# Last modes by column halves, moved identity passes, two more weight loads by fours, and 8 of 18 output items in 4 KB rows

## The chip, the cores and the metric

The kernel runs on one core of a Trainium2 chip. The core has five engines that follow their own instruction streams and wait for each other by semaphores: TensorE (PE, matrix products into the accumulators called PSUM), VectorE (DVE), ScalarE (ACT), GpSimd (POOL) and SyncE (SP). Transfers between device memory and on-chip memory run on 16 DMA engines; they are issued by instructions on the queues of POOL, SP or ACT. Here POOL issues nearly all loads, because they turn 32-bit inputs into 16-bit data on the way, and SP issues all stores. The metric is the device time in microseconds of one execution; less is better.

## The reference

Two parts follow each other. First a sparse attention over 8 batches, 8 heads, 576 positions and 64 columns per head. Heads 0 to 3 look at the last 32 positions, heads 4 to 7 at the earlier positions with the same remainder modulo 32:

```python
mask_local = (rel >= 0) & (rel < stride)
mask_strided = (rel >= 0) & (pos[None, :] % stride == pos[:, None] % stride)
...
attn = np.exp(scores)
attn = attn / (np.sum(attn, axis=-1, keepdims=True) + 1e-09)
return np.matmul(attn, v).astype(np.float32)
```

Its output, x with 8 x 576 rows of 512 columns, goes through a spectral mix. The first 64 Fourier modes of x along the positions are each multiplied by a complex 512 x 512 matrix of their own, the result y is added, and a last product with a positive part is added too:

```python
X = np.fft.rfft(x, axis=1)
Yr = np.einsum('bmd,mde->bme', Xr, w_r) - np.einsum('bmd,mde->bme', Xi, w_i)
Yi = np.einsum('bmd,mde->bme', Xr, w_i) + np.einsum('bmd,mde->bme', Xi, w_r)
Y[:, :n_modes] = Yr + 1j * Yi
y = np.fft.irfft(Y, n=S, axis=1)
u = x + y
return (u + np.maximum(u @ w_ch, 0.0)).astype(np.float32)
```

The mode matrices are 2 x 64 x 512 x 512 numbers of 32 bits, 134 MB of reading. The output is 9.4 MB.

## The kernel before, in words

**Order of work.** The program writes out the order of every engine by hand. Strided attention of all batches comes first, then local attention of all batches (a loop over b, L850), into which the first modes are woven: `NMODES` of them per batch, 14 with batch 0. Then comes a stretch with the other modes, and at the end the inverse transform and the output.

**Modes and their two halves.** A mode is computed in two passes, one over the channels of each attention half. `mode(slot, m)` (L618) does mode m of one half. Slot 0, and slot 1 up to mode 47, go in pairs through `mode_pair` (L589), with the weights streaming through PE (the matmuls of L601). The last 16 modes of slot 1 go singly with the weights held and X streaming: 16 matmuls of L634 per mode, four column blocks e times four channel blocks c. Eight modes share one PSUM bank `y`. When the bank is complete, `spectrum` (L563) adds it on DVE into the tile `YT` (L567); for the last bank this happens in two parts, after modes 61 and 63.

**Weights.** `w_fetch` (L161) issues the loads of mode weights on POOL: w_r into partitions 0 to 63, w_i into 64 to 127. The unit is a pair of modes, 512 KB for w_r and 512 KB for w_i. The pairs live in a ring `wring` with room for five; three of the first eight pairs (`GUEST`: 1, 2 and 7) live in other tiles and give no ring place back. A pair of numbers in the set `QUADS` (L153) is loaded with the following pair in one go (four modes, 1 MB each for w_r and w_i) as soon as two places are free; the set starts at 13. `UNEVEN` splits a few loads into row counts that spread differently over the DMA engines. A load waits on POOL until PE has used the weights whose place it takes, and POOL works in order. The eight first pairs are issued during strided attention. From then on each use of a pair that is in the ring calls w_fetch once.

**Tail.** With the last bank in YT, `spec_z` (L742) multiplies the last 16 modes by w_ch (four matmuls into zp; ACT copies it to `zzs`), and eight transposes bring the same modes into yp (DVE copies them to `yys`). Earlier modes have by then been folded into kept partial sums: v0s (product with w_ch) and xos (without), by `renew`. The output is made in 18 items k, each 512 KB. For an item, `v_early` (L994) and `u_early` (L1002) pass the kept sums through PE with an identity matrix into PSUM; `new_rows` (L1009) adds the last modes, by matmuls that use only 32 of the 128 rows of the PE array, row group b % 4 for batch b; `v_done` (L1036) takes the positive part on ACT; `u_done` (L1048) adds both on DVE and issues the store on SP. In items 4, 5 and 6 (`pooled`, L999) POOL adds one kept half in place of PE. The identity passes of items 0 and 1 (two v_early, one u_early) stand after mode 62, by `late[22]` (L1062).

**Items.** Items 0 to 15 take a pair of batches and one of four sets t of 128 rows: t % 2 is the parity of the row number, t // 2 the first or second half of the rows. A partition holds one row of 2 KB for each of the two batches, and a store writes rows of 2 KB that lie 4 KB apart (`out_rows`, L1022). Items 16 and 17 take the 64 remaining rows of four batches each. Items 0, 4, 5 and 6 are added and stored in two halves (`pieces`).

Of the kernel before, what the change touches and what calls it, by code (L numbers as in the profile page):

```python
# [10 lines left out]
FP = mybir.dt.float32  # L11
F16 = mybir.dt.float16
# [6 lines left out]
DM = 512  # L19
NM = 64  # L20
# [36 lines left out]
def kernel(  # L57
# [10 lines left out]
    nc = tc.nc  # L68
    PSUM = bass.MemoryType.PSUM
# [5 lines left out]
    pss = {}  # L75
# [10 lines left out]
    def psum(kind, half=False, pair=False):  # L86
        if pair:
            return pss[kind].tile([128, 2, 512], FP, tag=kind, name=kind)
        if half:
            return pss[kind].tile([128, 1024], F16, tag=kind, name=kind)  # L90
        return pss[kind].tile([128, 512], FP, tag=kind, name=kind)
# [19 lines left out]
    idn = cs["cI"]  # L111
# [6 lines left out]
    Xh = {1: big.tile([128, 4, B, 2, NM], F16, name="X1")}  # L118

    YS = {}  # L120
# [29 lines left out]
    ORDER = [(1, m) for m in range(SPLIT1)] + [(0, m) for m in range(SPLIT0)]  # L150
    ORDER += [(1, m) for m in range(SPLIT1, NM)] + [(0, m) for m in range(SPLIT0, NM)]
    UNEVEN = {64: (25, 12, 27), 84: (6, 54, 4), 94: (10, 54)}
    QUADS = {p for p in range(13, 54) if (p - 13) % 5 in (0, 2)}  # L153
    wring = pw.tile([128, 2 * NWBUF, 4, DM], F16, tag="w", bufs=1, name="wring")
    w_tiles = []
    w_chs = {}
# [4 lines left out]
    def w_fetch(n=1):  # L161
        free_pairs[0] += n
        while len(w_tiles) < 2 * NM:
            i = len(w_tiles)
            pair = i // 2
            nm = 4 if pair in QUADS else 2
            if 2 * free_pairs[0] < nm:
# [86 lines left out]
    def act_copy(out, in_):  # L254
        nc.scalar.activation(out=out, in_=in_, func=ACTF.Copy)  # L255
# [300 lines left out]
    ypt = {}  # L556
    queued = []

    def flush():
        while queued:  # L560
            queued.pop()()

    def spectrum(slot, part, src):  # L563
        if slot == 0:
            nc.scalar.activation(out=YS["Y0"][part], in_=src, func=ACTF.Copy)
        else:
            nc.vector.tensor_tensor(  # L567
                out=YS["YT"][part], in0=src, in1=YS["Y0"][part], op=AluOp.add
            )
# [48 lines left out]
    def mode(slot, m):  # L618
        half = 1 - slot
        if m % 2:  # L620
            flush()
        if slot == 0 or m < SPLIT0:
            if m % 2:
                mode_pair(slot, m - 1)
            return
        mi, mg = m % 8, m // 8
        if mi == 0:
            ypt[slot] = psum("y")
        yp = ypt[slot]
        yv = yp.rearrange("p (m e x) -> p m e x", m=8, e=4)  # L630
        wt = w_tiles[ORDER.index((half, m))]
        for e in range(4):
            for c in range(4):
                nc.tensor.matmul(  # L634
                    yv[:, mi, e, :],
                    wt[:, XC[c], ds(128 * e, 128)],
                    Xh[half][:, c, :, :, m],
                    start=(c == 0),
                    stop=(c == 3),
                )  # L640
        if m % 2:
            w_fetch()
        ends = {5: 6, 7: 2} if mg == 7 else {7: 8}
        if mi in ends:
            n = ends[mi]
            m0 = mi + 1 - n
            spectrum(
                slot,
                (slice(None), slice(None), mg // 2, slice(None), ds(8 * (mg % 2) + m0, n)),
                yp.rearrange("p (m e x) -> p e x m", m=8, e=4)[:, :, :, ds(m0, n)],  # L650
            )
# [90 lines left out]
    def spec_z(g, bq, zp):  # L742
        for e in range(4):
            lhs = YS["YT"][:, e, g, ds(8 * bq, 8), :].rearrange("p x m -> p (x m)")
            nc.tensor.matmul(
                zp, lhs, w_chs["n"][:, e, :], start=(e == 0), stop=(e == 3)
            )
# [56 lines left out]
    first = str_front(0)  # L804
# [45 lines left out]
    for b in range(B):  # L850
# [3 lines left out]
        ends = [lambda h=h: loc_scores(b, h, True) for h in (0, 2)]  # L854
# [8 lines left out]
        n = 0  # L863
        nm = NMODES[b]
        for mi in range(nm):
# [3 lines left out]
            n = upto  # L869
# [8 lines left out]
    zzs = [ptr.tile([128, DM], F16, name=f"zz{i}") for i in range(B)]  # L878
    yys = [ptr.tile([128, DM], F16, name=f"yy{i}") for i in range(B)]
# [22 lines left out]
    for b in range(B + 1):  # L902
        for t in range(5):
            if b > 0 and (t < 4 or b % 2 == 0):
                work.append(lambda b=b, t=t: premix(b - 1, t))
            if b < B and t < 4:
                half, cp = ((1, 0), (1, 1), (0, 0), (0, 1))[t]
# [3 lines left out]
    A3 = cs["cFl"].rearrange("p a t m -> p (a t m)")[:, 0 : S + 128]  # L911
# [25 lines left out]
    n = 0  # L937
    for m in range(SPLIT0):
# [4 lines left out]
        n = upto  # L943
# [7 lines left out]
    def spec_late(mm, kept, eng):  # L951
        up = psum("p", pair=True)
        for bq in range(2):
            mm(2, bq, up[:, bq])
        for b in range(B):
            eng(kept[b][64:96], up[ds(32 * (b % 4), 32), b // 4])
# [19 lines left out]
    late = {0: [lambda: spec_late(spec_z, zzs, act_copy)], 1: [spec_last]}  # L976
    for n, i in enumerate([3, 5, 7] + list(range(8, 21))):
        b, t = n // 2, n % 2 * 2
# [3 lines left out]

    items = []
    for P0 in (0, 2):
        items += [((2 * P, 2 * P + 1), t) for t in range(4) for P in (P0, P0 + 1)]
    items += [(range(b, b + 4), 4) for b in (0, 4)]
    LAST = len(items) - 1
    vps, ups, rls, osbs = {}, {}, {}, []

    def own(item, kept, half):  # L990
        bs, t = item
        return [kept[b][:, t] for b in bs] if t < 4 else [half[b // 2] for b in bs[::2]]

    def v_early(k):  # L994
        vps[k] = psum("p", pair=True)
        for j, r in enumerate(own(items[k], v0s, v0h)):
            nc.tensor.matmul(vps[k][:, j], idn, r, start=True, stop=False)  # L997
# [4 lines left out]
    def u_early(k):  # L1002
        ups[k] = psum(("p", "u")[k % 2], pair=True)
        for j, r in enumerate(own(items[k], xos, xoh)):
            if pooled(k, j):
                continue
            nc.tensor.matmul(ups[k][:, j], idn, r, start=True, stop=False)

    def new_rows(k, acc, spectra):  # L1009
        bs, t = items[k]  # L1010
        for j, b in enumerate(bs):
            q = ds(32 * (b % 4), 32)
            i = j // 2 if t == 4 else j
            o, cols = acc[:, i], row_cols(b, t)
            if t == 4:
                o = acc[ds(64 * (b % 2), 64), i]
            fresh = spectra is yys and pooled(k, i)
            nc.tensor.matmul(  # L1018
                o, A3[q, cols], spectra[b // 4][q], start=fresh, stop=True
            )  # L1020

    def out_rows(b, t):  # L1022
        if t < 4:
            steps = [[2 * DM, 128], [(S + 64) * DM, 2], [1, DM]]
            first = 256 * (t // 2) + t % 2
        else:
            steps = [[DM, 128], [2 * S * DM, 2], [1, DM]]
            first = 512
        return bass.AP(
            tensor=out.tensor, offset=out.offset + (S * b + first) * DM, ap=steps  # L1030
        )
# [14 lines left out]
                )  # L1046

    def u_done(k):  # L1048
        bs, t = items[k]
        up, rl = ups.pop(k), rls.pop(k)  # L1050
        if not osbs:
            osbs.append(pw.tile([128, 2 * NWBUF, 2, DM], FP, tag="w", bufs=1, name="osb"))
        osb = osbs[0][:, k % (2 * NWBUF)]
        for j in pieces(k):
            nc.vector.tensor_tensor(
                out=osb[:, j], in0=up[:, j], in1=rl[:, j], op=AluOp.add
            )
            nc.sync.dma_start(out_rows(bs[0], t)[:, j], osb[:, j])

    flush()  # L1060
    rest = [(0, m) for m in range(SPLIT1, NM)] + [(1, m) for m in range(SPLIT0, NM)]
    late[22] = [lambda: v_early(0), lambda: v_early(1), lambda: u_early(0)]  # L1062
    for i, (slot, m) in enumerate(rest):
        mode(slot, m)
        for w in late.get(i, ()):
            w()
    yctx.close()
    with tc.tile_pool(name="ps_s", bufs=1, space=PSUM) as pss["s"]:
        zp = pss["s"].tile([128, 512], FP, name="zp")
        yp = pss["s"].tile([128, 2, 512], F16, name="yp")  # L1070
        spec_z(3, 0, zp)
        act_copy(zzs[0], zp)
        for bq in range(2):
            for e in range(4):
                lhs = YS["YT"][:, e, 3, ds(8 * bq, 8), :].rearrange("p x m -> p (x m)")
                nc.tensor.transpose(yp[:, bq, ds(128 * e, 128)], lhs, idn)
        for bq in range(2):
            nc.vector.tensor_copy(out=yys[bq], in_=yp[:, bq])
    pss["u"] = pctx.enter_context(tc.tile_pool(name="ps_u", bufs=1, space=PSUM))

    for k in range(2):
# [1 line left out]
    for k in range(2):  # L1083
        v_done(k)
    for k in range(2):
        if k:
            u_early(k)
        new_rows(k, ups[k], yys)
        u_done(k)
    for k in range(2, LAST + 2):  # L1090
        if k == 7:
            held = psum("p", pair=True)[:, 0]
            spec_z(3, 1, held)
            act_copy(zzs[1], held)
        if k <= LAST:
            v_early(k)
        if k > 2:
            u_early(k - 1)
        if k <= LAST:
            new_rows(k, vps[k], zzs)  # L1100
        if k > 2:
            new_rows(k - 1, ups[k - 1], yys)
        if k <= LAST:
            v_done(k)
        if k > 2:
            u_done(k - 1)
# [31 lines left out]
```

## Time and profile before

| | |
|---|---|
| time, median of 3 runs | 425.84 us (425.5 to 427.29) |
| the profiled execution | 425.88 us, span 424.1 us |
| PE busy | 340.9 us (80%) |
| DVE busy | 234.6 us (55%) |
| ACT busy | 219.0 us (52%) |
| POOL busy | 95.7 us (23%) |
| software queue (POOL's loads) | 24624 packets, 81.28 MB, 96.7% of 16 engines' span |
| hardware queue (SP's stores and two small loads) | 5248 packets, 9.65 MB, 6.2% |
| stores | 14 of 512 KB and 8 of 256 KB |

How to read it. The profile is one execution. "Busy" is time in which an instruction of the engine ran. The page's slices cut the span into 40 equal parts. In the order of time a row is: start and duration in us, engine, line of the kernel, operation, tile written <- tiles read, shapes, count of merged instructions, and in brackets how long the engine had been idle before and what ended that. The windows table gives for each stretch the busy time of every engine, the granted share of PE's clock, the share of DMA engines at work and the GB/s that landed on chip (16-bit data; what is read from memory is twice that for the weights).

### The profile page before, as it was taken

Reading aid. Unit: us, or ns where it says so; the run is one execution under the profiler, and the core shown is the slowest. Engines: PE = TensorE matmul, PEld = TensorE weight load, DVE = VectorE, ACT = ScalarE, POOL = GpSimd, SP = SyncE. Lnnn points to the kernel's source line nnn. Section 1 sums busy time; section 2 is a strip of 40 time slices with the busy share of each in tenths; the row PEclk is TensorE's granted clock in tenths of the full one; section 3 lists DMA queues with packets and bytes.
Section 4 is the critical chain, followed back from the end, with each engine's and each line's share of the span. In section 5 each row is a group of like instructions: output and inputs, shape, how many; then the busy total and the mean of one; then the engine's idle time right before and its main releaser. Section 6 shows DMA issues by size and latency. Waiting matters only on the chain.

```text
span 424.1 us, 9718 instructions
## 1 busy us (share of the span) xinstructions
PE 340.9 (80%) x4164; PEld 206.5 (49%) x4164; DVE 234.6 (55%) x469; ACT 219.0 (52%) x391; POOL 95.7 (23%) x165
## 2 busy tenths in 40 slices
PE   2987878769999298889874959895779979989993
PEld 2866767554656155556542425453344534535331
DVE  3788788950354134545323326864385646555794
ACT  1687678642666056565753323622162365534772
POOL 7332333322422011102122101212111232310200
PEclk9999899967999789999998789999798998989999
DMA  8999999999999999999999999999999999997598
GB/s 147 211 212 213 213 212 214 210 212 210 214 214 211 215 216 213 214 215 214 211 215 213 212 211 216 213 213 214 213 214 211 214 214 214 213 213 145 196 380 316
DMA packets 30347, 91.62 MB, mean 216 GB/s; under 512 B 3873, under 2 KB 4641, under 8 KB 30305
## 3 DMA queue, kind: packets, MB, share of 16 engines
q0 software_dynamic: 24624, 81.28, 96.7%
q1 hardware_dynamic: 5248, 9.65, 6.2%
q8 instruction: 32, 0.52, 0.5%
q10 hardware_dynamic: 432, 0.08, 0.1%
q14 instruction: 11, 0.08, 0.0%
HBM read 162.83 MB, written 9.44 MB: 406 GB/s over the span
## 4 chain that ended last, share of the span: by engine, by line
PE 46%; DMA 23%; DVE 17%; ACT 8%; issue 4%; POOL 1%; DVEq 0%; ACTq 0%; POOLq 0%
DMA wring<-in_moe_w_i_dram 22%; PE y L601 11%; PE sc L726 5%; DVE xb L245 3%; ACT X L255 3%; DVE kz L287 3%; DVE yy L761 2%; PE p L997 2%; PE tp L417 2%; PE y L536 2%; PE sc L536 2%; PE sc L463 2%; PE p L769 2%; PE p L1018 1%; ACT PL L493 1%
## 5 line engine op out<-in xcount | busy, mean ns | idle before, releaser
L601 PE MATMUL y<-wring,X 128*32 128x512 f16 (+1 forms) x424 | 65.8, 422 | 23.6 <-DMA wring<-in_moe_w_i_dram 23.6
L190 POOL DMA_DIRECT2D wring<-in_moe_w_r_dram x39 | 23.6, 606 | 204.3 <-PE y L601 180.6
L601 PEld LDWEIGHTS <-X 128*32 128x32 f16 (+1 forms) x448 | 27.5, 139 | 41.4 <-DMA wring<-in_moe_w_i_dram 24.3
L735 ACT ACTIVATE v<-sc 128x512 f16<-128x512 f32 x32 | 19.1, 597 | 45.4 <-PE sc L726 45.4
L736 DVE COPY xo<-tp 128x512 f16<-128x512 f16 x32 | 22.1, 691 | 36.5 <-PE tp L734 36.4
L255 ACT ACTIVATE yr<-y 128x512 f16<-128x512 f32 x28 | 16.7, 597 | 41.2 <-PE y L601 41.0
L726 PE MATMUL sc<-w_cp,xT 128*128 128x512 f16 x128 | 36.2, 404 | 1.9 <-DVE xT L694 1.9
L245 DVE TENSOR_TENSOR xb<-av,rec 90x256 f16<-90x256 f32 (+2 forms) x80 | 36.0, 450 | 2.8
L493 ACT ACTIVATE PL<-sc 128x480 f16<-128x480 f32 (+1 forms) x48 | 26.9, 578 | 20.1 <-PE sc L479 19.8
L244 DVE RECIPROCAL rec<-av 90x4 f32<-90x4 f32 (+2 forms) x80 | 14.6, 183 | 39.3 <-PE av L508 28.2
L424 DVE COPY qT<-tp 128x576 f16<-128x576 f16 x16 | 11.9, 752 | 38.1 <-PE tp L417 38.1
L971 DVE TENSOR_TENSOR xo<-p,xo 128x1024 f16<-128x1024 f32 x16 | 19.6, 1225 | 14.3 <-PE p L769 14.3
L190 POOL DMA_DIRECT2D wring<-in_moe_w_i_dram x42 | 25.6, 609 | 6.1 <-DMA ring<-in_k_dram 2.0
L382 ACT ACTIVATE PL<-sc 90x360 f16<-90x360 f32 (+1 forms) x48 | 22.7, 490 | 7.1 <-PE sc L375 6.6
L255 ACT ACTIVATE v<-p 128x1024 f16<-128x1024 f32 x16 | 16.4, 1024 | 17.4 <-PE p L769 17.4
L255 ACT ACTIVATE v<-tp 128x640 f16<-128x640 f16 (+1 forms) x24 | 19.0, 807 | 11.6 <-PE tp L451 9.3
L417 PE MATMUL tp<-cI_s,ring 64*64 64x64 f16 x864 | 22.2, 196 | 2.7 <-DVE qT L424 2.4
L463 PE MATMUL sc<-cMl_s,cI_s 128*128 128x480 f16 (+1 forms) x48 | 18.9, 395 | 5.1 <-ACT PL L493 3.5
L280 PE MATMUL tp<-cI_s,ring 72*128 72x72 f16 x256 | 15.4, 207 | 9.1 <-DMA ring<-in_v_dram 7.4
L255 ACT ACTIVATE kz<-tp 64x360 f16<-64x360 f16 (+1 forms) x32 | 18.9, 592 | 6.2 <-PE tp L417 5.2
L417 PEld LDWEIGHTS <-ring 64*64 64x64 f16 x864 | 17.3, 109 | 9.0 <-issue 4.9
L536 PEld LDWEIGHTS <-xb 108*128 108x128 f16 (+2 forms) x176 | 15.4, 106 | 11.7 <-DVE xb L245 7.6
(146 smaller groups left out, 747.9 us busy)
## 6 DMA issues: line engine op xcount, KB each, us to landing
wring<-in_moe_w_r_dram POOLq DMA_DIRECT2D x17, 1024.0 KB, 13.3
wring<-in_moe_w_i_dram POOLq DMA_DIRECT2D x16, 1024.0 KB, 17.5
wring<-in_moe_w_i_dram POOLq DMA_DIRECT2D x24, 512.0 KB, 15.1
wring<-in_moe_w_r_dram POOLq DMA_DIRECT2D x22, 512.0 KB, 13.4
out_dram<-osb SPq DMA_DIRECT2D x14, 512.0 KB, 3.8
ring<-in_v_dram POOLq DMA_DIRECT2D x8, 288.0 KB, 13.3
ring<-in_q_dram POOLq DMA_DIRECT2D x8, 288.0 KB, 13.5
ring<-in_k_dram POOLq DMA_DIRECT2D x8, 288.0 KB, 13.1
```

The lines of the kernel that those rows point to most:

```text
L190: nc.gpsimd.dma_start(dst, rows)
L245: nc.vector.tensor_tensor(out=dst, in0=val.rearrange("p h (q c) -> p h c q", c=4), in1=rec[0:n, 0:pieces] .to_broadcast((n, pieces, 64)) . ...
L255: nc.scalar.activation(out=out, in_=in_, func=ACTF.Copy)
L382: nc.scalar.activation(out=PS[0:n, ds(POFF[t], 4 * n)], in_=scp[0:n, 0 : 4 * n], func=ACTF.Exp, scale=SCALE,)
L417: nc.tensor.transpose(tp[ds(64 * hp, 64), ds(64 * i, 64)], qn[ds(64 * hp, 64), ds(64 * (9 * g + i), 64)], idn[ds(64 * hp, 64), ds(64 * hp, ...
L463: nc.tensor.matmul(scp[:, 0 : n * times].rearrange("p (h x) -> p h x", h=times), idn, mask_rows("cMl", n, times), start=True, stop=False,)
L493: nc.scalar.activation(out=dst, in_=src, func=ACTF.Exp, scale=SCALE)
L536: nc.tensor.matmul(xp[:, ds(192 * cp, 192)].rearrange("p (f m) -> p f m", f=3), xb[b][0:n, base + t, ds(128 * cp, 128)], F[0:n, :, t, :], ...
L601: nc.tensor.matmul(yp[ds(a, 32), :], Xh[half][pr, c].rearrange("p b r (h m) -> p (b r h) m", h=2)[:, :, mm % 32], wt[pr, XC[c], :], start= ...
L726: nc.tensor.matmul(vp, xT[:, ch], w_chs["cp"][:, ch, :], start=(ch == 0), stop=(ch == 3),)
L736: nc.vector.tensor_copy(out=xo.rearrange("p (h q c) -> p h q c", h=2, c=4), in_=tp[:, 0:512].rearrange("p (h c q) -> p h q c", h=2, c=4),)
L971: nc.vector.tensor_tensor(out=xo, in0=up[:, 0:n], in1=xo, op=AluOp.add)
```

## The change

1. `QUADS` starts at pair 8 and not at 13, with the same pattern, so that pairs 8 and 9, and pairs 10 and 11, are each loaded in one go of four modes.
2. Modes 62 and 63 of the second slot write two PSUM banks of their own, one for column blocks 0 and 1, one for 2 and 3. After mode 63's matmuls of each half, `spectrum` adds that half for both modes.
3. After mode 62 only `v_early(1)` remains. `v_early(0)` goes behind `spec_z`, `u_early(0)` behind the `new_rows` of items 0 and 1. zp and yp take their banks from the pool of the `y` banks.
4. Of the items, those with t = 2 and t = 3 (second half of the rows, both parities) no longer take a pair of batches and one parity, but one batch and both parities. A partition then holds two rows that follow each other in the output, and the store writes 4 KB rows, in one piece per item. These are items 4 to 7 and 12 to 15. So that the two parities of one batch use different row groups of the PE array, `swap` makes copies of zzs and yys on POOL with the halves of the partitions exchanged, in the space of the tile X1, and `new_rows` reads the copy for t = 3. Six of the eight POOL copies are issued ahead of item 0, two at item 7.

```diff
-    QUADS = {p for p in range(13, 54) if (p - 13) % 5 in (0, 2)}
+    QUADS = {p for p in range(8, 54) if (p - 8) % 5 in (0, 2)}
...
+        if m == NM - 2:
+            ypt["last"] = [psum("y") for _ in range(2)]
+        if m >= NM - 2:
+            yl = [y.rearrange("p (m e x) -> p m e x", m=8, e=4) for y in ypt["last"]]
         wt = w_tiles[ORDER.index((half, m))]
         for e in range(4):
+            if m >= NM - 2:
+                yv = yl[e // 2]
             for c in range(4):
...
+            if m == NM - 1 and e % 2:
+                es = slice(e - 1, e + 1)
+                spectrum(
+                    slot,
+                    (slice(None), es, mg // 2, slice(None), ds(14, 2)),
+                    yv[:, ds(6, 2), es].rearrange("p m e x -> p e x m"),
+                )
         if m % 2:
             w_fetch()
-        ends = {5: 6, 7: 2} if mg == 7 else {7: 8}
+        ends = {5: 6} if mg == 7 else {7: 8}
...
-        items += [((2 * P, 2 * P + 1), t) for t in range(4) for P in (P0, P0 + 1)]
-    items += [(range(b, b + 4), 4) for b in (0, 4)]
+        items += [((2 * P, 2 * P + 1), (t, t)) for t in (0, 1) for P in (P0, P0 + 1)]
+        items += [((b, b), (2, 3)) for b in range(2 * P0, 2 * P0 + 4)]
+    items += [(range(b, b + 4), (4,) * 4) for b in (0, 4)]
...
-        bs, t = items[k]
-        for j, b in enumerate(bs):
-            q = ds(32 * (b % 4), 32)
+        for j, (b, t) in enumerate(zip(*items[k])):
+            g, src = b % 4, spectra[b // 4]
+            if t == 3:
+                g, src = (b + 2) % 4, other[spectra is yys, b // 4]
+            q = ds(32 * g, 32)
...
-                o, A3[q, cols], spectra[b // 4][q], start=fresh, stop=True
+                o, A3[q, cols], src[q], start=fresh, stop=True
...
+    def swap(spectra, i):
+        n = len(other)
+        kept = Xh[1].rearrange("p c b g m -> p (c b g m)")[:, ds(DM * n, DM)]
+        for p in (0, 64):
+            nc.gpsimd.tensor_copy(out=kept[ds(64 - p, 64)], in_=spectra[i][ds(p, 64)])
+        other[spectra is yys, i] = kept
...
     def out_rows(b, t):
-        if t < 4:
+        if t == 2:
+            first = 256 + 64 * (b % 2)
+            steps = [[2 * DM, 128], [1, 2 * DM]]
+        elif t < 4:
...
-            nc.sync.dma_start(out_rows(bs[0], t)[:, j], osb[:, j])
+            if ts[0] != 2:
+                nc.sync.dma_start(out_rows(bs[0], ts[0])[:, j], osb[:, j])
+        if ts[0] == 2:
+            nc.sync.dma_start(out_rows(bs[0], 2), osb.rearrange("p j x -> p (j x)"))
...
-    late[22] = [lambda: v_early(0), lambda: v_early(1), lambda: u_early(0)]
+    late[22] = [lambda: v_early(1)]
...
+    zp = psum("y")
+    yp = psum("y", half=True).rearrange("p (b x) -> p b x", b=2)
+    spec_z(3, 0, zp)
+    act_copy(zzs[0], zp)
+    v_early(0)
+    for bq in range(2):
+        for e in range(4):
+            lhs = YS["YT"][:, e, 3, ds(8 * bq, 8), :].rearrange("p x m -> p (x m)")
+            nc.tensor.transpose(yp[:, bq, ds(128 * e, 128)], lhs, idn)
+    for bq in range(2):
+        nc.vector.tensor_copy(out=yys[bq], in_=yp[:, bq])
+    swap(zzs, 0)
+    swap(yys, 0)
+    swap(yys, 1)
     yctx.close()
...
     for k in range(2):
-        if k:
-            u_early(k)
+        u_early(k)
         new_rows(k, ups[k], yys)
         u_done(k)
     for k in range(2, LAST + 2):
...
             act_copy(zzs[1], held)
+            swap(zzs, 1)
```

## The prediction, made before the changed kernel was run

> **What bounds the kernel now.** I read, in this order, the page's slices, the windows table, the order of time on GpSimd (POOL) and on TensorE (PE), and the order of time at the end. The slices say that this is a stream of loads with a tail:
>
> ```profile
> DMA  8999999999999999999999999999999999997598
> GB/s 147 211 212 213 213 212 214 210 212 210 214 214 211 215 216 213 214 215 214 211 215 213 212 211 216 213 213 214 213 214 211 214 214 214 213 213 145 196 380 316
> ```
>
> From the second slice to the 36th (10.6 us each) 210 to 216 GB/s land without a hole. The 81.3 MB of inputs set when the last weight arrives, whatever the engines do meanwhile. So a change ahead of 390 us matters only if it leaves the DMA engines without work. Loads are issued by POOL, which waits for PE to free a buffer. The windows table, and POOL's and PE's order of time:
>
> ```profile
> core 0: us, PE busy (x) PEld busy (x) DVE busy (x) ACT busy (x) POOL busy (x), PEclk, DMA share, GB/s
> 95.00:100.00 5.00, 4.65 (x15) 1.94 (x15) 0.00 (x0) 1.44 (x3) 1.62 (x3) 0.50 1.11 211
> 100.00:105.00 5.00, 4.29 (x38) 2.06 (x38) 0.69 (x2) 1.96 (x4) 1.20 (x2) 0.87 1.11 211
> 105.00:110.00 5.00, 4.99 (x82) 2.96 (x79) 2.21 (x4) 2.15 (x5) 1.17 (x2) 1.00 1.08 213
> ```
> ```profile
> 97.90 0.54 POOL L233 DMA_DIRECT2D ring<-in_k_dram  x1 [0.86 <-DMA ring<-in_v_dram]
> 101.10 0.60 POOL L190 DMA_DIRECT2D wring<-in_moe_w_r_dram  x1 [2.66 <-PE y L601]
> 101.70 0.60 POOL L190 DMA_DIRECT2D wring<-in_moe_w_i_dram  x1
> 107.70 0.58 POOL L190 DMA_DIRECT2D wring<-in_moe_w_r_dram  x1 [5.40 <-PE y L601]
> ```
> ```profile
> 97.04 3.76 PE L601 MATMUL y<-wring,X 64*32 64x512 f16 x8
> 106.32 1.08 PE L601 MATMUL y<-wring,X 128*32 128x512 f16 x8
> 120.82 1.08 PE L601 MATMUL y<-wring,X 128*32 128x512 f16 x8
> 128.27 1.08 PE L601 MATMUL y<-wring,X 128*32 128x512 f16 x8
> 147.66 0.65 PE L601 MATMUL y<-wring,X 128*32 128x512 f16 x2 [8.16 <-DMA wring<-in_moe_w_i_dram]
> ```
>
> At 97.90 the last attention input is issued. At 101.10 and 101.70 comes weight pair 8, released by pair 0 on PE (97.04 to 100.8), and not before 107.70 pair 9, released by pair 3 (106.32 to 107.40). PE had half its clock from 95 to 100.
>
> The tail, in order of time:
>
> ```profile
> 390.85 0.64 PE L634 MATMUL y<-X,wring 128*128 128x16 f16 x16
> 391.52 0.29 DVE L567 TENSOR_TENSOR YT<-y,Y 128x128 f16<-128x128 f32 x1 [1.90 <-PE y L634]
> 391.87 1.04 PE L745 MATMUL zp<-w_ch,YT 128*128 128x512 f16 x4 [0.39 <-DVE YT L567]
> 393.64 0.40 PE L1018 MATMUL p<-zz,cFl_s 32*128 32x512 f16 x4 [0.29 <-ACT zz L255]
> 395.42 24.03 SPq L1058 DMA_DIRECT2D out_dram<-osb  x22
> 399.98 3.38 POOL L1044 TENSOR_TENSOR rl<-rl,xo 128x512 f32<-128x512 f32 x3 [18.93 <-ACT rl L1041]
> ```
>
> Mode 63 starts at 390.85 because its last load, issued at 380.53, takes 10.1 us (390.63). Then come the spectra, and 18 output items of 512 KB. From 400.2 to 422.56 the output moves at 380 GB/s, 1.38 us an item, behind producers that need 1.295 (starts of PE's cycle 404.29, 405.58, 406.88).
>
> **Part 1: pairs 8 and 10 loaded by fours.** w_fetch now holds pair 8 until two pairs are free. Pairs 1 and 2 are guests that free nothing, so the load of 8 and 9 waits for pair 3, as pair 9 did: 107.70, and pair 8 loses its issue at 101.10. Behind it on POOL's queue stand pairs 10 and 11 (112.25, where pair 11 was), pair 12 (115.01) and the last attention inputs; none of them can pass.
> The queue is empty before that. The trace's transfer records say that the bytes of all loads issued through 97.90 have been moved by 106.84 (the 16 parts of that last load complete between 105.66 and 108.86). Restart after a dry queue is not shown in mid-kernel. From below: an output issued at 395.42 moves its first packet at 396.29, 0.87 us. From above: the kernel's first load, issued at 1.23, has its first packet at 2.91 and all engines running by 3.5 with a slow first packet, 2.6 in all. I take 1.9, near the first packet of the same queue (1.68). So the engines restart at 109.6 and stood still for 109.6 - 106.84 = 2.8 us (1.7 to 3.5). Nothing later gives it back, since no slice has a hole to fill. The 16 engines were 3.2 us apart at 107 and are 2.3 apart at the end; a common restart erases the first. If each kept its place the end would move by 1.4 only; if the ones ahead are the late ones at the end, up to 0.6 more than the mean. I take the mean.
> PE hardly notices: a pair of 1 MB transfers takes 9.8 us (4.90 each by the records, against 2.46 for 512 KB, so the larger size itself gains 0.02), pairs 8 and 9 land at 119.4 before their use at 120.82; pairs 10 and 11 land at 129.2, 0.9 after PE wants them at 128.27, and that is covered by the 8.16 us that PE waits at 147.66. If this cover were gone, 0.9 would be added to PE, not to the stream.
>
> **Part 2: column halves.** Eight matmuls of mode 63 take 0.32. The add of 64 elements is priced by two rows of L567, 128 elements 0.29 and 384 elements 0.55: 1.0 ns each, so 0.23. It runs beside the other eight matmuls, spec_z's first half beside the second add: spec_z starts at 391.51 and not at 391.87, 0.36 gained. Mode 62's wait for the old bank (0.53 at 389.08) is ahead of the landing and costs nothing either way.
>
> **Part 3: identity passes.** The six passes L997 and L1007 at 389.56 to 390.99 ran before the last weight was used, so they cost nothing. Two remain there. Four (v_early(0), u_early(0)) now stand behind spec_z: 4 x 0.215 = 0.86 on PE. PE was waiting there for zz (0.29 with the load ahead of it: 0.23 usable), so the third item, from which output is dense, comes 0.63 later after spec_z. With part 2: +0.27.
>
> **Part 4: the 4 KB items.** Six POOL copies 64x512 come ahead of the pooled adds: L333 copies 576 elements in 1.17, so 1.04 each, from 393.25 to 399.5; the first add wants POOL at 399.98 + 0.27. Hidden, by 0.75 us. Two more come after the adds, 3 us before use.
> The four matmuls of L1018 in one cycle run side by side (0.39 for four on different 32-row groups). With groups b and b+2, items 4, 8 and 12 share a group with the item before: 3 x 0.21 = +0.64 on PE by the last item.
> Transfers: an item is 16 packets of 2 KB on each of 16 engines, 1.376/16 = 86 ns each; an 8 KB read costs 306 ns (4.90/16), so a line through both gives 159 for 4 KB against 172: 8 items x 0.10 = 0.8 saved, as far as loads stand for stores; 0 saved at the other end. Here the Trainium skill (DMA: Bandwidth & Descriptors, "Why small descriptors are slow") counts about 3 cycles on top of one per 32 bytes: 67 per 2 KB and 131 per 4 KB, 2.2%, an estimate of 0.25 us; no run here shows it yet.
> But the last item is issued 0.27 + 0.64 later, 419.99. Undisturbed, 512 KB takes 2.3 us (second item: issued 397.35, moved by 399.65): 422.3, where it was 422.56. The queue alone would give 422.06 with the faster packets and 422.83 without. I take 422.45: -0.1 for parts 2 to 4 (-0.4 to +0.4).
>
> **Sum.** The profiled execution took 425.88 us (span 424.1 and 1.8 around it), 0.04 over the median of three, 425.84. 425.88 + 2.8 - 0.1 = 428.5, and 428.5 against the median is +0.6%. A measurement here can't tell less than 0.5% (2.1 us) from no change.
>
> **Rivals.**
> A, forecast: the dry queue, 428.5. Its own range 427.0 to 430.2 (1.4 to 4.1 us, less the tail). Chance 0.55.
> B, PE is earlier, so the queue never runs dry (the other side: no change). From 91 to 101.3 PE ran at half clock: L536 2.1, L463 and L479 1.7, pair 0 3.7. At full clock half of these 7.5 goes, pair 3 is done at 103.7, the load is issued near 104.0 and moves at 105.9, before 106.84. It decides from 2.8 us earlier on. Then 425.8. For it: the next window has 1.00. Against: PE idled around 90 (1.7 us) and 94.5 (1.6 us), and these idle times are the kernel's own. The Trainium skill (TensorE: Matmul & The Clock Gate, Part 1) says that the gate's 3.4 us window runs free of the kernel's start, so that slow stretches shift from run to run; the rows of half clock here lie on such a grid. Chance 0.25.
> C, the half clock lasts one window (3.4 us) longer: 1.7 more of work at half speed, so 430.2. Chance 0.1.
> D, POOL's copies cost 1.5 (contention, strided rows): nine us, the first pooled add comes 2 us late, and DVE, which adds in order, holds every later item. Decides from 1.17 us a copy. With 0.4 to 1.1 us of queued output as cover: 429.7. Against: the same L333 row. Chance 0.05.
> E, the tail gives more than I take (0.8 from the packets, 0.36 from the halves, conflicts hidden) and nothing runs dry: 425.88 - 1.2 = 424.7, or under 423.7 if the stores gain twice as much. Chance 0.05.
>
> **Numbers.** Faster: the far end of E and some of B's spread, 0.05. Same (to 428.0): B, half of E, and under a third of A, 0.42. Slower: the rest of A, C, D, 0.53. The range takes in B below and C above: 425.2 to 430.4.
>
> **What would show it.** A slice near 107 with the GB/s cut by about a quarter, POOL's first 64x4x2048 load at 107 to 108 with PE as its releaser, the last weight landing 2.8 us later. In the tail: spec_z 0.66 after mode 63's start (before 1.02), first matmuls of L1036 0.2 later after spec_z, last output issued 0.6 later after mode 63. Wrong if the slices near 107 have no hole (B), if POOL's adds start late (D), or if the output runs well over 380 GB/s (E).

## The result, and the profile after

The changed kernel takes 430.48 us (median of six runs, 429.01 to 431.22) against 425.82 for the kernel before, measured beside it (six runs, 425.0 to 427.29). The ratio is 1.0102, with a 95% interval of 1.0077 to 1.0127: 1.0% slower. The forecast was 428.5, also slower, with a range of 425.2 to 430.4; the median lies 0.1 above that range, and the ratio times the 425.84 of the prediction (430.2) just inside. So the sign and the first cause were right, and about 2 us were not seen.

The profiled execution took 429.01 us, the fastest of the six. Its slices (10.7 us each), on the page of the changed kernel:

```profile
DMA  8999999999999999999999999999999999997498
GB/s 149 211 214 213 212 214 212 211 210 200 179 215 212 213 215 212 214 212 214 211 214 213 212 214 214 214 204 207 210 212 209 213 213 214 212 214 158 180 376 329
```

The tenth and eleventh slices, 96 to 118 us, have fallen from 210 and 214 GB/s to 200 and 179: the forecast hole is there. The windows table of the changed kernel shows its place, and POOL's order of time what stands around it:

```profile
core 0: us, PE busy (x) PEld busy (x) DVE busy (x) ACT busy (x) POOL busy (x), PEclk, DMA share, GB/s
95.00:100.00 5.00, 5.00 (x16) 1.66 (x14) 0.00 (x0) 1.14 (x2) 1.62 (x3) 0.50 1.11 212
100.00:105.00 5.00, 4.29 (x50) 2.45 (x49) 0.78 (x3) 1.96 (x4) 0.00 (x0) 0.99 1.11 209
105.00:110.00 5.00, 4.99 (x90) 3.36 (x90) 2.76 (x7) 2.54 (x5) 1.25 (x2) 1.00 0.75 118
110.00:115.00 5.00, 5.00 (x62) 3.00 (x59) 1.07 (x4) 3.86 (x9) 2.31 (x4) 1.00 1.05 210
```
```profile
97.69 0.54 POOL L233 DMA_DIRECT2D ring<-in_k_dram  x1 [0.86 <-DMA ring<-in_v_dram]
106.60 0.63 POOL L190 DMA_DIRECT2D wring<-in_moe_w_r_dram  x1 [8.37 <-PE y L601]
107.22 0.63 POOL L190 DMA_DIRECT2D wring<-in_moe_w_i_dram  x1
111.15 0.61 POOL L190 DMA_DIRECT2D wring<-in_moe_w_r_dram  x1 [3.31 <-PE y L601]
```

After the last attention input (97.69) nothing is issued for 8.37 us; before the change a load stood at 101.10. The load of pairs 8 and 9 comes at 106.60 with PE as its releaser, and between 105 and 110 the DMA engines are at work for 0.75 instead of 1.08, and 118 GB/s land instead of 213. By the transfer records the stream is level with that of before at 20 MB (0.18 us ahead) and 2.03 us behind at 22 MB. It loses 0.4 more up to 270 us, 0.9 between 270 and 310 us, where the slices show 204 to 212 GB/s, and 0.2 after that. The last weight lands at 393.86 instead of 390.35.

The tail of the changed kernel, in order of time:

```profile
394.32 0.64 PE L640 MATMUL y<-X,wring 128*128 128x16 f16 x16 [0.60 <-DMA wring<-in_moe_w_i_dram]
394.76 0.46 DVE L567 TENSOR_TENSOR YT<-y,Y 128x64 f16<-128x64 f32 x2 [1.32 <-PE y L640]
395.04 1.04 PE L758 MATMUL y<-w_ch,YT 128*128 128x512 f16 x4
396.83 1.28 POOL L1046 COPY X<-zz 64x512 f16<-64x512 f16 x2 [11.72 <-issue]
396.88 0.40 PE L1036 MATMUL p<-zz,cFl_s 32*128 32x512 f16 x4
398.17 2.61 POOL L1046 COPY X<-yy 64x512 f16<-64x512 f16 x4
403.68 3.47 POOL L1074 TENSOR_TENSOR rl<-rl,xo 128x512 f32<-128x512 f32 x3 [2.91 <-ACT rl L1071]
```

spec_z (L758) starts 0.72 after mode 63 (L640), where it was 1.02 (391.87 - 390.85). A POOL copy takes 0.64 (1.28 for two), and POOL then waits 2.91 for its first add. The output ends at 425.97 by the transfer records, 31.65 after mode 63's start, where it was 422.56 - 390.85 = 31.71. So this execution says: stream +3.51, tail -0.10 counted from the last landing, and 0.28 less after the last output byte; together +3.13, the 429.01 against 425.88.

That is not the whole result. The other five runs took 430.1 to 431.2, and none of them was traced. A second profile of the same kernel (e13, below) shows what this execution happened not to have: TensorE at half its clock over the front of the tail.

### The profile page after: what moved, and what is told of

Its sections match the earlier page's. It is cut to its first block, busy times and chain, and to the rows that moved or that the text cites. A ratio compares the mean times of both kernels' runs of the same rounds, so it can differ in the third digit from the quotient of the medians.

```text
span 427.2 us, 9714 instructions
## 1 busy us (share of the span) xinstructions
PE 340.5 (80%) x4164; PEld 205.8 (48%) x4164; DVE 235.1 (55%) x470; ACT 219.2 (51%) x391; POOL 98.4 (23%) x169
## 5 line engine op out<-in xcount | busy, mean ns | idle before, releaser
L190 POOL DMA_DIRECT2D wring<-in_moe_w_r_dram x37 | 22.5, 609 | 212.7 <-PE y L601 189.2
L190 POOL DMA_DIRECT2D wring<-in_moe_w_i_dram x40 | 24.3, 609 | 8.4 <-DMA wring<-in_moe_w_i_dram 3.9
L1071 ACT ACTIVATE rl<-p 128x1024 f32<-128x1024 f32 (+1 forms) x19 | 18.4, 979 | 5.9 <-PE p L1036 4.4
```

The lines of the kernel that those rows point to most:

```text
L190: nc.gpsimd.dma_start(dst, rows)
```

## The experiments

All ratios are to runs of the kernel before on the same chip, with 95% intervals.

**e1: the loads by fours taken back.** The changed kernel with

```diff
-    QUADS = {p for p in range(8, 54) if (p - 8) % 5 in (0, 2)}
+    QUADS = {p for p in range(13, 54) if (p - 13) % 5 in (0, 2)}
```

> The changed kernel with the set of fours starting at pair 13 again; the halves, the moved passes and the 4 KB items stay. If the load of pairs 8 and 9, held until pair 3, is the whole loss (the queue theory), the hole near 107 us goes and the time is that of the kernel before less what the tail gained: 425.5 us, 425.0 to 426.3. If the tail carries part of the loss (its passes behind the last load, POOL's copies), it stays 1 us or more above the kernel before, over 426.8.

427.87 us, 1.0043 (1.0028 to 1.0058). 2.6 of the 4.7 us went. About 1.8 us over the kernel before were left, where the prediction's terms for parts 2 to 4 add up to -0.1. The profile of e1, front of the tail, in order of time and as windows that follow the steps in which the granted clock changes (columns as above):

```profile
390.52 0.64 PE L640 MATMUL y<-X,wring 128*128 128x16 f16 x16 [1.45 <-DMA wring<-in_moe_w_i_dram]
391.24 1.23 PE L758 MATMUL y<-w_ch,YT 128*128 128x512 f16 x4
392.26 1.06 PE L1013 MATMUL p<-v,cI_s 128*128 128x512 f16 x2
393.11 1.06 PE L1108 MATMUL y<-cI_s,YT 128*128 128x128 f16 x8
```
```profile
388.50:391.91 3.41, 1.88 (x27) 0.95 (x24) 0.45 (x2) 0.00 (x0) 0.00 (x0) 1.00 0.12 23
391.91:395.32 3.41, 3.41 (x18) 1.42 (x16) 0.76 (x2) 1.17 (x3) 1.83 (x3) 0.51 0.00 0
395.32:398.74 3.42, 3.42 (x19) 0.92 (x18) 2.42 (x3) 2.46 (x4) 1.84 (x3) 0.99 0.34 126
```

PE idles for 1.45 us ahead of mode 63, since four of the six identity passes are no longer there to be done. In the 3.41 us up to 391.91 it is busy for 1.88, and the next 3.41 us have half the clock: the two passes of L1013 take 1.06 (0.59 at full clock), the eight transposes of L1108 1.06 (before 0.61). The output ends 33.62 after the last landing; it was 32.21 in the kernel before and 32.11 in the first profile of the changed kernel.

**e2: the loads by fours alone.** The kernel before with the change's line:

```diff
-    QUADS = {p for p in range(13, 54) if (p - 13) % 5 in (0, 2)}
+    QUADS = {p for p in range(8, 54) if (p - 8) % 5 in (0, 2)}
```

> The kernel before with the set of fours starting at pair 8, and nothing else. Queue theory: a hole of 2 to 3 us near 107 us, no work for the DMA engines, and 429.5 to 431 us, so the whole loss and a little more. If the tail carries the loss: within 1 us of the kernel before.

429.03 us, 1.0079 (1.006 to 1.0099), 2.9 us by the medians and 3.4 by the ratio. In its profile the load of pairs 8 and 9 comes at 105.93, the stream loses 1.8 from 20 to 22 MB and its last weight lands 3.1 later than before, and the tail is that of before (32.17 from landing to the output's end, 32.21 before). Part 1 alone costs about 3 us.

**e3: another load in the hole.** The changed kernel with w_ch's 512 KB, which stood ahead of batch 6, issued at the start of the loop:

```diff
-        if b == 6:
+        if b == 0:
             work.insert(0, w_ch_fetch)
```

> The changed kernel, with the load of w_ch (512 KB, 2.46 us of the engines, issued at 198 us in the kernel before) issued already ahead of the load of pairs 8 and 9, with no wait on PE. Queue theory: it fills the hole, the engines move bytes that they would move later anyway, and the time falls by 2.0 to 2.5 us against the changed kernel, to about 428 us; a remainder of the hole of 0 to 1 us stays where the clock is late. If loads by fours cost something by their size or by the order of their semaphores, w_ch changes nothing: 430 to 431 us.

428.56 us, 1.0051 (1.0026 to 1.0076). w_ch is issued at 98.27, the load of pairs 8 and 9 at 106.70 as late as in the changed kernel, and the stream is 0.01 later at 22 MB instead of 2.03. So the late issue costs nothing while the queue has other work: the dry queue is the cost. The scatter is wide (425.45 to 432.61); the profiled execution, 429.61, has half clock from 391.9 to 398.8, two steps, and its output ends 34.62 after the last landing.

**e4: one load by four alone.** The kernel before with pair 10 added to the set, so that 10 and 11 go by four and 8 doesn't:

```diff
-    QUADS = {p for p in range(13, 54) if (p - 13) % 5 in (0, 2)}
+    QUADS = {p for p in range(13, 54) if (p - 13) % 5 in (0, 2)} | {10}
```

> The kernel before, with pairs 10 and 11 loaded in one go and pair 8 issued at 101 us as before. There are as many waits and the same size of load as for pair 8, but the queue then holds 9 us of work. Queue theory: within 0.4 us of the kernel before. If a load by four costs by itself: 1 us or more above it.

426.17 us, 1.0004 (0.9989 to 1.002). A load of four as such costs nothing; what costs is holding pair 8.

**e5: the passes back, too.** e1 with the six passes after mode 62 again; halves and 4 KB items remain.

```diff
-    late[22] = [lambda: v_early(1)]
+    late[22] = [lambda: v_early(0), lambda: v_early(1), lambda: u_early(0)]
...
-    v_early(0)
...
-        u_early(k)
+        if k:
+            u_early(k)
```

> As e1_quads_back, but with all six identity passes of items 0 and 1 ahead of mode 63 again, so that the column halves and the 4 KB items remain of the change. If moving the passes is what the tail lost, the time falls from e1's 427.9 us to that of the kernel before or a little below: 425.3 us, 424.8 to 426.2. If the 4 KB items or the copies on POOL cost it, it stays over 426.8.

425.81 us, 0.9987 (0.997 to 1.0004). Against e1 the passes' place is worth 2.06 us by the medians and 2.4 by the ratios, and the tail of its profile is 31.71 from landing to the output's end, at full clock.

**e6: matmuls in the idle stretch.** e1 with six 128x512 matmuls that nothing reads between modes 62 and 63. The passes stay where the change put them.

```diff
+    def warm(n):
+        vps[0] = psum("p", pair=True)
+        for i in range(n):
+            nc.tensor.matmul(vps[0][:, 0], idn, v0s[0][:, 0], start=True, stop=True)
...
-    late[22] = [lambda: v_early(1)]
+    late[22] = [lambda: v_early(1), lambda: warm(6)]
```

> As e1_quads_back (passes late), plus six matmuls 128x512 between modes 62 and 63 whose result nobody reads; all else, the four passes behind spec_z too, stays. Clock theory: with the passes gone PE idles before the last load and gets half its clock for the first 3.4 us of the tail; the filler keeps it busy, the slice after mode 63 shows a granted clock of 1.00 and the time falls by about 1 us, to 426.3 to 427.2. Count theory (the prediction's): the four passes cost their 0.86 us wherever the clock is; six more matmuls change nothing or add, 427.9 or more.

426.9 us, 1.0012 (0.9989 to 1.0035), from e1's 1.0043. The profiled execution was the slowest (429.84), since its stream was late by then (last landing 394.74). Its tail, in order of time:

```profile
395.15 0.64 PE L640 MATMUL y<-X,wring 128*128 128x16 f16 x16 [0.19 <-DMA wring<-in_moe_w_i_dram]
395.87 1.04 PE L758 MATMUL y<-w_ch,YT 128*128 128x512 f16 x4
```

PE waits 0.19 instead of 1.45 ahead of mode 63, the clock is 1.00, spec_z takes 1.04 instead of 1.23, and landing to output end is 32.05 instead of 33.62. Work for nothing makes the tail 1.6 us shorter in the traces and the median about 1 us lower; the intervals of e1 and e6 still overlap.

**e7: the passes moved alone.** The kernel before with the move of part 3 and nothing else; `v_early(0)` stands behind the copy into `zzs[0]`.

```diff
-    late[22] = [lambda: v_early(0), lambda: v_early(1), lambda: u_early(0)]
+    late[22] = [lambda: v_early(1)]
...
+        v_early(0)
...
-        if k:
-            u_early(k)
+        u_early(k)
```

> The kernel before with only the identity passes moved as in the change; no halves, no 4 KB items, no fours. Clock theory: 1.5 to 2.2 us above the kernel before, 427.4 to 428.1, with half the clock behind mode 63 in the profile. Count theory: 0.6 us above it (0.86 less the wait for zz), 426.5.

428.61 us, 1.0054 (1.0036 to 1.0072): +2.5 by the medians (426.07 before in these runs), +2.3 by the ratio. That is above even the 427.4 to 428.1 of the clock theory. The profiled execution was among its fastest (427.42) and does not show the cost: its half clock falls at 378.5 to 385.3, PE comes to mode 63 late by itself (392.29, 1.57 after the landing), and from there to the output's end it takes 31.78 against 31.71 before, at full clock. That does not mean that the order is free: the last store is issued 28.70 after mode 63 and not 28.23, 0.47 later, and then takes 3.09 to its last byte instead of 3.49. The last store of kernels with 2 KB items alone took 3.09 to 3.90 in the traces; whether the 0.40 is this scatter, or stores queued ahead of it that left less to wait for, is not shown.

**e8: the items alone.** e5 without the column halves; one bank and one add for mode 63 as before.

```diff
...
-            if m == NM - 1 and e % 2:
-                es = slice(e - 1, e + 1)
...
-        ends = {5: 6} if mg == 7 else {7: 8}
+        ends = {5: 6, 7: 2} if mg == 7 else {7: 8}
```

> As e5_passes_early without the column halves, so that only the 4 KB items with their copies on POOL remain of the change. By the prediction's sum: -0.25 to +0.4 us (faster packets against shared row groups), 425.6 to 426.4. The difference to e5 is the worth of the halves, 0.36 us by the prediction's sum. A loss over 1 us would say that the copies on POOL or the single stores are what the tail lost.

426.01 us, 0.9992 (0.9976 to 1.0007); e5 has 0.2 less, which is not to be told from nothing.

**e9: matmuls in PE's idle stretches around 88 us, with the loads by fours alone.** e2 with

```diff
+        if b == 0 and hh == 0:
+            for i in range(24):
+                nc.tensor.transpose(tv[:, 7, :], idn, idn)
...
-    for w in front1[:4]:
+    for w in front1[:3]:
+        w()
+    warm("sc", 6)
+    front1[3]()
     dft(B - 1, 1)
+    warm("av", 6)
```

The transposes stand at the head of `loc_back`; `warm` runs 128x512 matmuls into a spare bank.

> Before with the loads by fours from pair 8 alone, and with idle stretches of PE filled by matmuls that nothing reads: 24 transposes ahead of the wait at 81 us, six 128x512 matmuls in each of the waits at 88 and 92 us. Without the fillers this edit gave 1.0079, with half clock from 83.5 to 100.6 us. Theory (the hole is PE's lateness: rival B of the prediction decides by the clock): the granted clock stays 1.00 or loses less than one window, pair 3 ends at 104 and not at 106, the load of pairs 8 and 9 is issued 2 us earlier, the slice near 107 keeps 205 GB/s or more, and the ratio falls to 0.999 to 1.003. Rival (a load of four costs by itself, or the queue runs dry anyway because the issue can't come before the buffers' other use): the clock is full and the ratio stays at 1.006 to 1.010. If the fillers don't hold the clock, the run tells neither.

426.91 us, 1.0016 (1.0005 to 1.0026), from e2's 1.0079. Windows table and POOL's order of time of e9:

```profile
95.00:100.00 5.00, 4.47 (x38) 2.41 (x35) 0.69 (x2) 1.63 (x3) 1.62 (x3) 1.00 1.11 210
105.00:110.00 5.00, 4.99 (x76) 3.27 (x72) 2.31 (x6) 2.83 (x5) 1.70 (x3) 1.00 1.10 210
```
```profile
98.08 0.54 POOL L233 DMA_DIRECT2D ring<-in_k_dram  x1 [0.87 <-DMA ring<-in_v_dram]
104.30 0.63 POOL L190 DMA_DIRECT2D wring<-in_moe_w_r_dram  x1 [5.68 <-PE y L604]
104.92 0.63 POOL L190 DMA_DIRECT2D wring<-in_moe_w_i_dram  x1
```

The clock from 95 to 100 is 1.00 and not 0.50, the load is issued at 104.30, and the slice of 105 to 110 has its 210 GB/s. The prediction's rival B had said 104.0 for full clock.

**e11: the passes back, the loads by fours kept.** The changed kernel with e5's diff only.

> The changed kernel with its six identity passes back after mode 62, loads by fours from pair 8 kept: only part 3 is undone. Theory (two costs that add: the dry queue 2.9 us, and the idle PE ahead of the last load with the half clock that follows, 1.7 to 2.3 us): 425.8, as measured without either, plus 2.9, so 428.7 (1.0068; 1.005 to 1.009), with spec_z at full clock in the profile. Rival (the two don't add, because the later end of the stream already pays for the later tail, or the difference is scatter from run to run): 430.0 or more (1.0095 and above), as the whole change.

428.94 us, 1.0072 (1.0052 to 1.0092). With e1, e5 and the changed kernel this makes a table of two causes; the two add, within the scatter:

| | passes early | passes moved | |
|---|---|---|---|
| QUADS from 13 | 425.81 (e5) | 427.87 (e1) | +2.1 |
| QUADS from 8 | 428.94 (e11) | 430.48 (changed kernel) | +1.5 |
| | +3.1 | +2.6 | |

These medians come from different chips. Taken as differences to the kernel before on the same chip, they give 2.01 and 1.77 for the passes, and 3.15 and 2.91 for the loads.

**e12: the whole change, with the clock kept up.** Nothing undone; the matmuls of e9 and those of e6 added:

```diff
...
+    keep("sc", 6)
+    front1[3]()
     dft(B - 1, 1)
+    keep("av", 6)
...
-    late[22] = [lambda: v_early(1)]
+    late[22] = [lambda: v_early(1), lambda: warm(6)]
```

> The changed kernel with nothing undone and only PE's idle stretches filled by matmuls that nothing reads: 24 transposes and two times six 128x512 matmuls between 81 and 94 us, and six 128x512 matmuls between modes 62 and 63. Theory (both costs of the change come through the granted clock): the load of pairs 8 and 9 is issued near 104 and no slice near 107 is below 205 GB/s, spec_z runs at full clock, and the ratio falls from 1.0102 to between 1.000 and 1.005 (427.2 from 425.8 + 0.7 for the first filler's measured rest + 0.7 for the second's). Rival (one of the costs is in the order of the work and not in the clock): 1.007 or more for the dry queue alone, 1.005 to 1.007 for the passes alone.

426.53 us, 1.0005 (0.9995 to 1.0016). The full 4.7 us are gone. The slices of e12, then its POOL and PE rows:

```profile
GB/s 153 211 214 212 214 212 213 211 211 208 213 213 213 214 214 215 213 215 215 211 215 213 214 214 213 215 210 212 209 214 208 213 214 213 215 211 143 211 377 302
```
```profile
103.88 0.63 POOL L190 DMA_DIRECT2D wring<-in_moe_w_r_dram  x1 [6.03 <-PE y L604]
```
```profile
391.07 0.64 PE L643 MATMUL y<-X,wring 128*128 128x16 f16 x16
391.79 1.04 PE L761 MATMUL y<-w_ch,YT 128*128 128x512 f16 x4
```

No slice near 107 has a hole (208 and 213), the load comes at 103.88, mode 63 waits for nothing and spec_z runs at full clock (1.04). Its output ends 32.89 after the last landing, later than 32.11, though every store is issued as in the first profile of the changed kernel: the last one alone takes 3.49 instead of 2.69 from issue to its last byte. Why is not shown.

**e13: a second profile of the changed kernel,** with no edit.

> The changed kernel once more, for its tail: the profiled execution at 429.01 was the fastest of six, the others took 430.1 to 431.2. Theory (the slower ones carry half clock over the front of the tail): if this execution takes 430 or more, its granted clock is 0.50 in the windows after mode 63 and the output ends 33.5 to 34.7 us after the last load has landed, where the first look had 32.1; if it takes 429, the clock there is 1.00 and the distance 32.1. Rival (the slower ones are late in the stream): the distance is 32.1 at 430 or more, and the last load lands after 394.8.

431.55 us, one execution. Its windows at the tail, and spec_z:

```profile
391.97:395.38 3.41, 1.61 (x22) 0.69 (x22) 1.61 (x3) 0.60 (x1) 0.00 (x0) 1.00 0.59 117
395.38:398.79 3.41, 3.06 (x22) 1.44 (x23) 0.45 (x2) 0.50 (x1) 0.00 (x0) 0.51 0.00 0
```
```profile
395.64 0.64 PE L640 MATMUL y<-X,wring 128*128 128x16 f16 x16 [1.39 <-DMA wring<-in_moe_w_i_dram]
396.36 1.89 PE L758 MATMUL y<-w_ch,YT 128*128 128x512 f16 x4
```

PE is busy for 1.61 of 3.41 us, and then spec_z takes 1.89 instead of 1.04 at a clock of 0.51. The expectation is met in part: the distance from landing to output end is 33.30, a little under its 33.5, and the rival holds as well, since the last load lands at 395.18. The load of pairs 8 and 9 was issued at 107.43 here, 0.83 later than in the first profile. Of the 2.54 us between the two executions, 1.32 are in the stream and 1.19 in the tail.

**The tail taken apart.** The traces agree to 0.01 us on when the last store is issued, counted from mode 63's start, as long as the clock is full. So this time separates what the medians blur:

| tail | granted clock behind mode 63 | last store issued after mode 63's start, us |
|---|---|---|
| as before (before, e2, e9; e4 0.01 more) | full | 28.23 |
| passes moved (e7) | full | 28.70 |
| 4 KB items (e8) | full | 28.92 |
| 4 KB items, halves (e5, e11) | full | 28.62 |
| all three (first profile of the changed kernel, e6, e12) | full | 28.96 |
| all three (e13) | half for one step of 3.41 us | 30.17 |
| all three (e1) | half for one step | 30.54 |
| all three (e3) | half for two steps | 31.53 |

The items add 0.69, the halves take 0.30 away, the new order of the passes adds 0.34 (with the other parts) or 0.47 (alone), and half clock adds 1.21 to 2.57 on top. From issue to last byte the last store takes 2.66 to 2.69 in the kernels with 4 KB items, but for e12's 3.49, and 3.09 to 3.90 in the others.

**Which version is best.** None beats the kernel before by more than these runs can tell; e5 (0.9987, up to 1.0004) comes nearest.

## Why the prediction was right in its sign and short in its size

**Part 1, the dry queue (+2.8): right.** Hole, releaser and place came as written. Alone it costs 2.9 to 3.4 (e2). What was not foreseen is how exactly it hangs on the issue time. The loss of the stream between 20 and 22 MB, by transfer records, to about 0.1 us:

| kernel | pairs 8 and 9 issued at, us | stream later by, us |
|---|---|---|
| e12 | 103.88 | 0.3 |
| e9 | 104.30 | 0.1 |
| e2 | 105.93 | 1.8 |
| e11 | 106.30 | 2.2 |
| changed kernel, first profile | 106.60 | 2.2 |
| e13 | 107.43 | 3.2 |
| e3, w_ch in the hole | 106.70 | 0.3 |

Each microsecond of a later issue is about one of stream, from some 104.3 on. The prediction took the 107.70 of the trace of before as the issue time, 1.1 later than it came, and a restart of 1.9; with 106.60 its own sum gives 106.60 + 1.9 - 106.84 = 1.7, and 2.2 was lost. So the issue was put too late by 1.1 and the restart too short by about 0.5, and the hole as such came out 0.6 smaller than the 2.8. That the whole cost of part 1 is near 2.8 all the same is in part luck: the four executions with the hole (e2, e11, e13 and the first profile) lose 0.5 to 2.1 us more between 22 MB and their last landing, and the prediction has no term for that. Such late losses come in executions without this part too (e6: slices of 198 and 191 GB/s), so they don't need it; whether it makes them more frequent, and what they are, stays open.

**Rival B (clock up, no hole): wrong as a forecast, right as a mechanism.** None of the profiles without added matmuls shows it. With them, e9 and e12, the hole closes at the issue time that B gave. B's weight of 0.25 on chance was too much: the idle stretches ahead are the kernel's own, as the prediction itself argued.

**Part 2, column halves (-0.36): right.** spec_z starts 0.30 sooner after mode 63 in the changed kernel (0.72 against 1.02), 0.06 less than written, and the last store is issued 0.30 sooner in e5 than in e8. In time it is the 0.2 between e5 and e8, not to be told from nothing.

**Part 3, the moved passes (+0.63, with part 2 +0.27): the step that failed.** The prediction wrote: "The six passes L997 and L1007 at 389.56 to 390.99 ran before the last weight was used, so they cost nothing." True, but they also kept PE busy. With four of them gone, PE idles 1.4 us ahead of mode 63 in e1, e3 and e13 (0.60 in the first profile), and in these three half clock follows over spec_z, the transposes and the first items. Measured: +2.3 to +2.5 alone (e7), +2.1 and +1.5 in the table, where the step's own sum was 0.63. The order as such, which is what that 0.63 priced, costs 0.34 to 0.47 by the issue of the last store at full clock, and in the changed kernel as much by the output's end (31.65 after mode 63's start, 31.30 in e5 and e11). The clock, which the prediction put at nothing here, costs 1.21 to 2.57 in the three traces that have it, so it is the larger part. That it is the clock is shown by e6 and e12, where added matmuls keep it full with the passes left in their new place: their last store is issued at 28.96 and not at 30.17 to 31.53. In the medians e6 gives back 1.0 of e1's 2.1; its runs scatter from 425.24 to 429.84. How often half clock falls into the tail is not known, since only one execution of a run is traced. The prediction knew the mechanism: rivals B and C are about the clock at 100 us, and the same view shows PE's rows at 390. It was not asked what the removed work did for the clock there.

The Trainium skill (TensorE: Matmul & The Clock Gate, Part 1) says that the gate judges PE's activity over windows of 3413 ns that run free of the kernel. The rows agree: the half clock comes and goes in steps of 3.41 us, and they lie differently in the executions (from 391.9 in e1, from 395.4 in e13, none in the tail of the first profile). So the cost of an idle stretch varies from run to run, 0 to 2.5 us here (32.11 to 34.62 from landing to output end).

**Part 4, the 4 KB items (0.8 saved in transfers, +0.64 on PE, copies hidden): right.** A packet of 4 KB takes 163 ns, one of 2 KB 87 (transfer records; the estimate from the 8 KB reads was 159 against 86), so an item of 512 KB takes 8 x 163 = 1.30 us per engine and not 16 x 87 = 1.39. With the items alone (e8) the last store is issued 0.69 later after mode 63, where the shared row groups were put at 0.64. In the whole change it is issued 28.96 after mode 63 and not 28.23, 0.73 later, where the sum's terms gave 0.91 and its list of signs 0.6. From there it takes 2.69 to its last byte and not 3.49, so the two cancel as written (31.65 against 31.71 to the output's end). A copy costs 0.64 and not 1.04, which leaves rival D no ground.

The Trainium skill (DMA: Bandwidth & Descriptors, "Why small descriptors are slow") counts about 3 cycles on top for each packet, which makes the larger one cheaper by an estimated 2.2%. The records show 163 against 2 x 87 = 174, 6%, so the measurement decides for a fixed cost of 11 ns a packet.

**Sum.** +2.9 (e2), +2.1 or +1.5 (passes) and -0.3 (e5: halves and items) give 4.1 to 4.7; measured 4.7.

## What to carry to other kernels

An instruction that fills a wait has two values, its own work and the clock that it keeps up for what comes next. Before such work is moved behind the wait, look at what TensorE then does in the 3 to 4 us ahead of the critical stretch, and price that stretch at half clock. And a load that must wait for more room is free only while the queue ahead of it still holds work: compare its issue time with the time at which the queue runs dry, microsecond by microsecond.

## What the runs showed of the hardware that was not expected

- A wait much shorter than 3.4 us can be enough for half clock: it was 1.39 (e13) and 1.45 us (e1). The steps ahead of one were busy for 1.61 (e13) and 1.88 (e1) of 3.41 us; with 2.73 busy, in the changed kernel's first profile, the clock stayed. The way back wants more: in e3 a step with 2.85 busy at half clock was followed by another at half clock, in e13 one with 3.06 by full clock. The windows row of the first profile, and two of e3 that answer to e13's above:

```profile
393.63:397.04 3.41, 2.73 (x35) 1.68 (x34) 0.50 (x3) 0.60 (x1) 0.21 (x1) 1.00 0.00 0
```
```profile
391.89:395.30 3.41, 2.85 (x22) 1.38 (x23) 0.45 (x2) 0.29 (x1) 0.00 (x0) 0.51 0.00 0
395.30:398.71 3.41, 3.41 (x19) 1.22 (x18) 0.76 (x2) 1.76 (x4) 2.61 (x5) 0.50 0.00 0
```

All 14 traces, cut from 25 us on at such steps, say the same with a wide band between. Of the steps at full clock, the 60 in which PE was busy for less than 1.5 us were all followed by half clock, and none of the 1172 with 2.35 us or more was; of the 157 between, 65 were. Of the steps at half clock, none of the 86 with less than 2.9 us busy was followed by full clock; of the 140 with more, 122 were. So PE's busy time in a step bounds what comes next, but does not decide it alone.

- The time between the last output byte and the end of the execution is 3.02 to 3.07 us in the profiles with 4 KB items and 19 stores, and 3.31 to 3.36 in those with 22 stores. No run tells whether the number of stores makes this 0.3 us.
